# One core, cosine attention and a two-layer product: the hand-written order of steps is permuted from the start to the third batch's second unit

## The chip, the cores and the metric

The kernel runs on one core of a Trainium2 chip. The core has a matrix engine (TensorE, PE in the profile; its loads of weights are PEld), three engines for elementwise work (VectorE: DVE, ScalarE: ACT, GpSimd: POOL), and SyncE (SP), which here only issues DMAs. The metric is device time of one execution in microseconds (us). Three runs of the kernel before took 415.35 us in the median.

## The reference, cut to what matters

```python
q_n = q / (np.linalg.norm(q, axis=-1, keepdims=True) + 1e-06)      # q, k, v: (8, 12, 448, 64) float32
k_n = k / (np.linalg.norm(k, axis=-1, keepdims=True) + 1e-06)
scores = np.matmul(q_n, k_n.transpose(0, 1, 3, 2)) / tau           # tau = 0.1
attn = np.exp(scores - max); attn = attn / (sum(attn) + 1e-09)
x = np.matmul(attn, v).transpose(0, 2, 1, 3).reshape(3584, 768)
h = x @ w_in                                                       # (768, 2048)
out = np.maximum(0.01 * h, h) @ w_out                              # (2048, 768)
```

Eight batches, each with twelve heads of 448 rows and 64 columns; then a product with w_in, a leaky relu and a product with w_out over all 3584 rows.

## The kernel before, in words

The whole kernel is a list of steps, the string `ORDER` (lines 16 to 98). Each step is a name and numbers; a loop (L727) calls one small function for each step, and this function issues its instructions to its engine. Each engine takes its instructions in the order in which they were issued, and waits at each one until its inputs are there and its buffers are free. So `ORDER` fixes one queue for each engine. The relative order of two steps matters only where they are on one engine, or where they take a buffer from one pool.

A *pair* `s` is two heads of one batch (pairs 0 to 5 are batch 0, pairs 6 to 11 batch 1). From pair 12 on, work goes by *units*, and `s` counts the queries and the keys of a unit by turns: 12 and 13 are unit 0, 16 and 17 unit 2.

The steps of a pair, with engine and line:

- `lq.s` (SP, L222) loads queries and keys of a pair; pairs 0 to 5 are loaded ahead of the list (L651 to L659), from SP and, for three loads, ACT. Four buffers hold later pairs, in the order in which `lq` stands in the list. `hs.s` (SP, L700) is a tiny DMA that reads the normalised pair `s` and so holds SP's later DMAs back until `no.s` is done.
- `sq.s.p` squares (POOL, L306 and L300), part 0 the queries, part 1 the keys; for pair 0 and pair 1 ACT does it (`qf` L324, `sa` L304). `su.s.p` sums over columns (DVE, L319, L316; `uf` L330 for pair 0). `ro.s` is a log and an exponential that make a root (ACT, L336, L337). `no.s` normalises into bfloat16 (DVE, L342, L343, L359; L349 from pair 12).
- `tp.s` transposes (PE, L374), `tc.s` copies the result (DVE, L390); for pair 0 in two parts, of which ACT copies one (`ta`).
- `k.s.i` scores (PE, L427), i from 0 to 2; `k.s.3` takes the last 64 keys of pairs s-1 and s together. `x.s.i` is their exponential (ACT, L438).
- Two pairs make a `j`: `to.j` sums the exponentials (PE, L450 with ones), `ln.j` and `in.j` make the inverse (ACT, L462, L466), `pr.j.e` multiplies with the values (PE, L450), `sc.j.e` scales into `xT` (DVE, L478).

For a unit the steps are `tt`, `td` (turned by DVE and spread by six SP DMAs, L400 and L409), `q` and `y` (scores and exponentials, L492 and L500), `g`, `gl`, `gi`, `gx` (sums or products, log, inverse, scaling: L538, L546, L550, L564 and L570).

The products with the weights go by chunks `c` of rows: chunk 0 is 384 rows of batch 0, chunk 1 the other 512 rows of batches 0 and 1. `f.c.m` multiplies with 128 columns of w_in (PE, L588, six matmuls, one for each 128 rows `kt` of w_in; `f.0.1.0.2` does only kt 0 and 2). Rows kt 0 and 1 come from j = 0, 2 and 3 from j = 1, 4 and 5 from j = 2. `r.c.m` is the leaky relu (ACT, L602). `s.c.t.lo.hi` multiplies 128 rows with half of w_out (PE, L624, sixteen matmuls), `o` copies the result (DVE, L640) and, when a row is complete, issues its DMA on SP.

POOL issues the other loads: `wi.i` (L182) a quarter of w_in, 0 and 1 the left half of the columns (m 0 to 7; 0 the even kt, 1 the odd), 2 and 3 the right half; `wo` (L188) w_out, first its left half of columns, then the right half in two quarters; `lv.j` and `lr` the values of batches 0 and 1 (L256, L264); `lg` the values of later groups (L282). `hp.s` (L704) is a tiny copy on POOL that reads the normalised pair `s` and so holds POOL's queue until `no.s` is done; `hr` (L707) waits in the same way for the first load.

PE writes into eight PSUM banks, given out when the list is walked (`take`, L156): the free bank that was given back longest ago. Scores take two banks, everything else one, except `g` with two. Until the step `tg` scores may only have banks 0 to 3 and the rest only 4 to 7; behind it all may have all eight. `w.n` (L695) is n matmuls on a constant tile, whose results nobody reads.

Of the kernel before, what the change touches and what calls it, by code (L numbers as in the profile page):

```python
# [21 lines left out]
k.3.1 x.3.1 pr.0.1 w.2 su.5.0 no.4 lq.9 su.5.1 sc.0.0 hp.4 sq.6.0 sq.6.1 wi.2 k.3.2 x.3.2 w.2 ro.5 tp.4 tc.4  # L22
k.3.3 x.3.3 w.2 k.4.0 x.4.0 k.4.1 x.4.1 to.1 ln.1 in.1 no.5 sc.0.1 hp.5 sq.7.0 sq.7.1 wi.3 k.4.2 x.4.2 tp.5
tc.5 pr.1.0 k.5.0 x.5.0 k.5.1 x.5.1 pr.1.1 sc.1.0 sc.1.1 su.6.0 su.6.1 su.7.0 su.7.1 wo.0 sq.8.0 sq.8.1 lv.3
lr.1.0.4 k.5.2 x.5.2 f.0.0.0.2 f.0.1.0.2 k.5.3 x.5.3 f.0.0.1 f.0.1.1 f.0.0.3 f.0.1.3 tg ro.6 to.2 ln.2 in.2
no.6 pr.2.0 pr.2.1 f.0.2.0.1.2.3 f.0.3.0.1.2.3 sc.2.0 sc.2.1 ro.7 lq.10 sq.9.0 sq.9.1 tp.6 tc.6 f.0.0.4.5
r.0.0 f.0.1.4.5 r.0.1 f.0.2.4.5 r.0.2 f.0.3.4.5 r.0.3 no.7 lq.11 su.8.0 su.8.1 k.6.0 k.6.1 k.6.2 x.6.0 x.6.1
x.6.2 f.0.4 r.0.4 f.0.5 r.0.5 tp.7 tc.7 ro.8 no.8 hp.8 sq.10.0 sq.10.1 lv.4 wo.1.0.8 su.9.0 su.9.1 f.0.6 r.0.6
f.0.7 r.0.7 k.7.0 k.7.1 x.7.0 x.7.1 f.0.8 r.0.8 tp.8 tc.8 ro.9 no.9 hs.9 lq.12 su.10.0 su.10.1 f.0.9 r.0.9
f.0.10 r.0.10 k.7.2 k.7.3 x.7.2 x.7.3 f.0.11 r.0.11 tp.9 tc.9 ro.10 no.10 hp.10 sq.11.0 sq.11.1 wo.1.8 lv.5  # L30
# [734 lines left out]
```

## Time and profile before

| | |
|---|---|
| median of three runs | 415.35 us (414.4 to 415.75) |
| the profiled execution | 415.95 us, with a span of 414.0 us |
| mean granted clock of PE | 1.000 |
| PE busy in the span | 403.3 us |
| DVE, ACT, POOL busy | 261.5, 247.3, 113.6 us |
| DMA | 53.81 MB |

The profile is of one execution. A row of a timeline gives start, duration, engine, line, operation and tiles; "[0.34 <-DVE ...]" is how long the engine was idle before it and what ended this. Times count from the start of the span. A window row gives the busy time of each engine in a stretch. Queue q0 carries the DMAs that POOL issues, q1 those of SP.

### The profile page before, as it was taken

Reading aid. Unit: us, or ns where it says so; the run is one execution under the profiler, and the core shown is the slowest. Engines: PE = TensorE matmul, PEld = TensorE weight load, DVE = VectorE, ACT = ScalarE, POOL = GpSimd, SP = SyncE. Lnnn points to the kernel's source line nnn. Section 1 sums busy time; section 2 is a strip of 40 time slices with the busy share of each in tenths; the row PEclk is TensorE's granted clock in tenths of the full one; section 3 lists DMA queues with packets and bytes.
Section 4 is the critical chain, followed back from the end, with each engine's and each line's share of the span. In section 5 each row is a group of like instructions: output and inputs, shape, how many; then the busy total and the mean of one; then the engine's idle time right before and its main releaser. Section 6 shows DMA issues by size and latency. Waiting matters only on the chain.

```text
span 414.0 us, 11078 instructions
## 1 busy us (share of the span) xinstructions
PE 403.3 (97%) x4662; PEld 211.0 (51%) x4679; DVE 261.5 (63%) x424; ACT 247.3 (60%) x431; POOL 113.6 (27%) x125
## 2 busy tenths in 40 slices
PE   7699999999999999999999999999999999999997
PEld 2235555544555555544455555554455555554465
DVE  6878878656678565765584877599978591310021
ACT  5897877288657786667864769525854735104400
POOL 4785564133235132432240623330010000000000
PEclk9999999999999999999999999999999999999999
DMA  7999999964387842693555756392052210010032
GB/s 184 234 203 220 218 222 201 257 166 114 62 212 193 209 112 56 181 232 98 96 136 159 178 154 165 79 206 83 2 90 78 87 40 0 2 70 7 2 114 76
DMA packets 41976, 53.81 MB, mean 130 GB/s; under 512 B 12486, under 2 KB 32326, under 8 KB 41926
## 3 DMA queue, kind: packets, MB, share of 16 engines
q1 hardware_dynamic: 25734, 41.01, 35.8%
q0 software_dynamic: 15504, 11.80, 19.7%
q8 instruction: 36, 0.59, 0.6%
q10 hardware_dynamic: 688, 0.30, 0.2%
q14 instruction: 14, 0.11, 0.1%
HBM read 45.61 MB, written 11.01 MB: 137 GB/s over the span
## 4 chain that ended last, share of the span: by engine, by line
PE 83%; DMA 6%; DVE 3%; issue 2%; ACT 2%; POOL 2%; SPq 1%; POOLq 0%; DVEq 0%
PE ps L624 33%; PE ps L588 32%; PE ps L538 7%; PE ps L492 6%; DMA qk_h<-in_k_dram 3%; PE ps L450 2%; DMA vq<-in_v_dram 2%; DVE qn L359 1%; DVE ss L319 1%; ACT pe L438 1%; DMA xT<-in_q_dram 1%; PE ps L427 1%; POOL sq L306 1%; SPq L409 1%; PE ps L524 1%
## 5 line engine op out<-in xcount | busy, mean ns | idle before, releaser
L624 PE MATMUL ps<-w_out_sb,hT 128*128 128x384 bf16 (+1 forms) x912 | 151.7, 324 | 0.0
L588 PE MATMUL ps<-xT,w_in_sb 128*128 128x384 bf16 (+1 forms) x753 | 150.3, 352 | 1.0 <-issue 0.3
L500 ACT ACTIVATE pe<-ps 128x896 bf16<-128x896 f32 x126 | 109.2, 917 | 46.8 <-PE ps L492 46.6
L624 PEld LDWEIGHTS <-hT 128*128 128x128 bf16 x912 | 86.4, 98 | 64.4 <-issue 10.7
L588 PEld LDWEIGHTS <-w_in_sb 128*128 128x128 bf16 x768 | 72.9, 98 | 73.5 <-issue 9.0
L602 ACT ACTIVATE hT<-ps 128x384 bf16<-128x384 f32 (+1 forms) x128 | 65.0, 552 | 62.3 <-PE ps L588 44.1
L300 POOL TENSOR_TENSOR sq<-qk_h 128x896 f32<-128x896 f32 x36 | 62.5, 1740 | 60.1 <-DMA qk_h<-in_k_dram 33.6
L640 DVE COPY osb<-ps 128x384 f32<-128x384 f32 (+1 forms) x57 | 30.7, 544 | 76.5 <-PE ps L624 72.9
L349 DVE TENSOR_TENSOR qn<-qk_h,r 128x896 bf16<-128x896 f32 x36 | 42.7, 1186 | 1.6 <-DVE r L343 0.4
L316 DVE TENSOR_REDUCE ss<-sq 128x14 f32<-128x910 f32 x36 | 38.1, 1062 | 1.1 <-POOL sq L300 1.1
L438 ACT ACTIVATE pe<-ps 128x896 bf16<-128x896 f32 x42 | 36.0, 917 | 3.2 <-PE ps L427 3.1
L492 PE MATMUL ps<-qkT 64*32 64x448 bf16 x1008 | 36.0, 352 | 0.3 <-DVE osb L640 0.3
L508 DVE TENSOR_TENSOR shared<-shared,pe 128x896 f32<-128x896 f32 x30 | 35.6, 1218 | 0.3
L564 DVE TENSOR_TENSOR xT<-ps,rb 128x448 bf16<-128x448 f32 x32 | 18.3, 614 | 20.3 <-ACT rb L550 12.4
L400 DVE STREAM_TRANSPOSE tt<-qn 128x448 f32<-128x448 f32 x36 | 29.3, 817 | 0.7
L704 POOL CAST seen<-qn 128x1 f32<-128x1 bf16 x21 | 3.9, 185 | 92.0 <-DVE qn L349 86.0
L342 DVE TENSOR_REDUCE r<-norms 128x14 f32<-128x28 f32 x48 | 8.4, 176 | 31.1 <-ACT norms L337 30.8
L538 PE MATMUL ps<-pe,vq 64*32 64x448 bf16 x1008 | 27.0, 349 | 0.0
L492 PEld LDWEIGHTS <-qkT 64*32 64x32 bf16 x1008 | 12.6, 91 | 19.2 <-issue 15.0
L336 ACT ACTIVATE ss<-ss 128x14 f32<-128x14 f32 x48 | 10.3, 215 | 18.3 <-DVE ss L316 17.2
L282 POOL DMA_DIRECT2D vq<-in_v_dram x20 | 12.7, 639 | 26.6 <-PE ps L492 26.6
L538 PEld LDWEIGHTS <-vq 64*32 64x32 bf16 x1008 | 14.6, 93 | 8.6 <-issue 0.6
(55 smaller groups left out, 234.9 us busy)
## 6 DMA issues: line engine op xcount, KB each, us to landing
qk_h<-in_q_dram SPq DMA_DIRECT2D x36, 224.0 KB, 4.1
qk_h<-in_k_dram SPq DMA_DIRECT2D x36, 224.0 KB, 4.1
out_dram<-osb SPq DMA_DIRECT2D x20, 384.0 KB, 2.6
qkT<-tt SPq DMA_DIRECT2D x72, 56.0 KB, 2.0
qkT<-tt SPq DMA_DIRECT2D x36, 112.0 KB, 2.6
vq<-in_v_dram POOLq DMA_DIRECT2D x16, 224.0 KB, 4.9
w_in_sb<-in_moe_w_in_dram POOLq DMA_DIRECT2D x4, 768.0 KB, 10.9
out_dram<-osb SPq DMA_DIRECT2D x15, 192.0 KB, 3.1
```

Source lines behind the costliest of these rows:

```text
L300: gp.tensor_tensor(sq[:, :, :D], x, x, op=ALU.mult)
L316: nc.vector.tensor_reduce(o, sqs[s], axis=AX.X, op=ALU.add)
L349: nc.vector.tensor_tensor(qn[s].rearrange("p m d e -> p m e d"), raw[s].rearrange(f"p ({t[1:-1]} d) -> p m e d", e=n, d=D), r.rearrange(f" ...
L438: nc.scalar.activation(out=dst, in_=sc[:, :, :S], func=AF.Exp, scale=inv_tau)
L492: nc.tensor.matmul(out=sc[32 * strip : 32 * strip + 32, a, :S], lhsT=x[rows, c0 : c0 + 32], rhs=x[rows, 0:S], start=True, stop=True,)
L500: nc.scalar.activation(out=pq[u, i], in_=sc[:, :, :S], func=AF.Exp, scale=inv_tau)
L508: eng.tensor_tensor(whole[u], pq[u, 0] if i == 1 else whole[u], pq[u, i], op=ALU.add)
L538: nc.tensor.matmul(out=po[32 * strip : 32 * strip + 32, w, :S], lhsT=weights, rhs=pq[us[x if two else 0], i][rows, a, :], start=(i == 0), ...
L588: nc.tensor.matmul(out=pm[:, :n], lhsT=w_in_sb[:, kt, m * 128 : (m + 1) * 128], rhs=xT[c // 2][:, kt, c0 : c0 + n], start=(done + i == 0), ...
L602: nc.scalar.activation(out=hT[c][:, m, :n], in_=pm[:, :n], func=AF.Prelu, alpha=0.01)
L624: nc.tensor.matmul(out=po2[:, : hi - lo], lhsT=hT[c][:, m, ts * 128 : (ts + 1) * 128], rhs=w_out_sb[:, m, lo:hi], start=(m == 0), stop=(m ...
L640: nc.vector.tensor_copy(out=o[:, lo:hi], in_=bank(("s", c, ts, lo))[:, : hi - lo])
```

## The change

Only the string `ORDER` changes. It holds the same 1261 steps, in another order from its first line up to `q.3.2` (the third batch's second unit is the one whose first score steps stand there); behind that point both lists are the same, but for one copy, `o.1.0.384.768`, which moves down to that border. The main moves:

- `tg` moves from the first products with w_in to the first transposes of pair 0.
- POOL: `sq.2` now stands in front of `lr.0` and `lv.0`; `hr` moves behind `lv.2`, `hp.1` behind `sq.4.1`; `lv.1` and the squares of pairs 3 and 4 stand in front of `wi.0` and `wi.1`, which follow each other; `wi.2` and `wi.3` follow each other behind the squares of pair 7; the last quarter of w_out stands behind `sq.13` and `sq.12`.
- SP: `lq.8` stands in front of `hs.3`; `lq.13` in front of `lq.12`; the order behind is `lq.16`, `lq.18`, `lq.19`, `lq.17`.
- ACT and DVE: the parts of pairs are taken in another order, `ro.1` stands in front of `ta.0.0.4`, `no.9` in front of `no.8`, some sums in front of norms that stood ahead of them.
- PE: `f.0.6` and `f.0.15` come forward, the steps `f.1` are mixed, `s.0.2.384.768` stands in front of `s.0.1.384.768`, and some steps of one kind that were apart now follow each other.

The diff, cut to the parts of which the prediction speaks:

```diff
-w.20 qf.0.0.3 uf.0.0.3 qf.1.0.3 uf.1.0.3 qf.0.3.4 uf.0.3.4 ro.0 hr lr.0.0.2 sa.1.1 sa.1.0 no.0 su.1.1 lq.6
-sq.2.0 sq.2.1 lv.0 tp.0.0.4 ta.0.0.4 tp.0.4.7 su.1.0 tc.0.4.7 w.3 ro.1 k.0.0 x.0.0 k.0.1 x.0.1 w.2 no.1 su.2.0
-su.2.1 lq.7 hp.1 sq.3.0 sq.3.1 lr.0.2.4 wi.0 k.0.2 x.0.2 ro.2 tp.1 tc.1 w.2 k.1.0 x.1.0 k.1.1 x.1.1 w.2 no.2
-su.3.0 sq.4.0 sq.4.1 lv.1 wi.1 k.1.2 x.1.2 w.2 tp.2 tc.2 k.1.3 x.1.3 su.3.1 ro.3 w.2 k.2.0 x.2.0 k.2.1 x.2.1
-to.0 ln.0 in.0 su.4.0 no.3 hs.3 lq.8 sq.5.0 sq.5.1 lv.2 su.4.1 k.2.2 x.2.2 tp.3 tc.3 pr.0.0 ro.4 k.3.0 x.3.0
...
+qf.0.0.3 qf.1.0.3 uf.0.0.3 lq.6 qf.0.3.4 w.20 uf.1.0.3 uf.0.3.4 ro.0 sa.1.1 sq.2.1 sa.1.0 no.0 tp.0.4.7 su.1.0
+sq.2.0 su.1.1 tg tp.0.0.4 w.2 lr.0.0.2 ro.1 tc.0.4.7 su.2.1 lv.0 sq.3.1 no.1 su.2.0 w.2 ta.0.0.4 sq.3.0 lq.7
+k.0.1 lr.0.2.4 x.0.1 k.0.0 w.2 w.2 tp.1 k.0.2 x.0.0 w.2 tc.1 k.1.3 ro.2 no.2 su.3.0 su.3.1 x.0.2 k.1.2 x.1.3
+lv.1 k.1.1 x.1.2 x.1.1 ro.3 w.2 sq.4.1 k.1.0 tp.2 w.3 tc.2 k.2.1 k.2.2 k.2.0 x.1.0 su.4.1 to.0 x.2.2 pr.0.0
+no.3 hp.1 sq.4.0 su.4.0 x.2.1 x.2.0 ro.4 tp.3 w.2 wi.0 tc.3 ln.0 wi.1 sq.5.1 k.3.3 lq.8 su.5.1 k.3.2 k.3.1
+sq.5.0 w.2 no.4 su.5.0 hp.4 sq.6.0 x.3.3 lv.2 hr x.3.1 x.3.2 pr.0.1 tp.4 tc.4 k.3.0 ro.5 x.3.0 no.5 in.0 k.4.0
+k.4.1 hp.5 x.4.1 sc.0.0 sc.0.1 to.1 tp.5 k.4.2 ln.1 pr.1.1 pr.1.0 sq.6.1 sq.7.0 sq.7.1 tc.5 x.4.0 in.1 x.4.2
+sc.1.1 k.5.0 sc.1.0 k.5.2 hs.3 x.5.0 k.5.3 wi.2 x.5.2 f.0.1.0.2 f.0.0.0.2 k.5.1 x.5.1 wi.3 su.6.0 su.6.1
+su.7.1 f.0.1.1 f.0.1.3 f.0.0.1 ro.6 x.5.3 sq.8.0 wo.0 lv.3 f.0.2.0.1.2.3 f.0.3.0.1.2.3 to.2 pr.2.1 pr.2.0 lq.9
+ln.2 in.2 no.6 su.7.0 tp.6 sq.8.1 lq.10 sc.2.1 sc.2.0 f.0.6 sq.9.1 f.0.3.4.5 f.0.2.4.5 f.0.0.4.5 r.0.6
+f.0.1.4.5 ro.7 lr.1.0.4 r.0.2 sq.9.0 tc.6 su.8.0 su.8.1 no.7 k.6.2 k.6.0 r.0.3 f.0.4 f.0.5 x.6.2 sq.10.0 tp.7
+lq.11 sq.10.1 tc.7 r.0.1 su.9.0 su.9.1 f.0.0.3 f.0.7 r.0.4 x.6.0 r.0.5 r.0.0 ro.8 f.0.15 k.6.1 k.7.0 ro.9
...
+tp.8 r.0.13 r.0.11 lq.13 r.0.12 wo.1.0.8 r.0.14 k.9.1 tc.8 x.9.1 su.11.1 sq.13 k.9.0 to.3 su.11.0 ln.3 lq.12
+k.9.3 ro.11 k.8.0 x.9.3 x.9.0 x.8.0 tp.10 s.0.0.0.384 no.11 tc.10 k.8.1 k.10.1 k.8.2 sq.12 x.8.1 in.3 pr.3.1
+o.0.0.0.384 wo.1.8 hs.11 su.13 pr.3.0 ro.13 x.8.2 x.10.1 tp.11 s.0.1.0.384 hp.11 tc.11 k.11.0 sc.3.0 lv.5
...
```

More of the change, by code (lines that the diff above doesn't have):

```diff
@@ L22 @@
[L22 to L26, printed above, removed]
@@ new lines @@
+y.1.5 r.1.8 g.0.0 r.1.14 q.2.0 q.1.6 su.21 su.20 s.1.0.0.384 y.1.6 ro.20 ro.21 y.2.0 gx.0.0 q.2.2 q.2.1 q.2.3
+no.21 o.1.0.0.384 tt.19 no.20 lq.22 tt.20 s.1.1.0.384 s.1.0.384.768 tt.21 lq.23 td.3 lq.24 td.4 lq.25
+o.1.1.0.384 sq.23 hp.19 sq.22 y.2.2 lg.1 su.22 y.2.1 q.2.4 y.2.3 hp.20 y.2.4 q.2.5 q.2.6 y.2.5 y.2.6
+s.1.1.384.768 o.1.1.384.768 ro.22 s.1.2.0.384 o.1.2.0.384 no.22 tt.22 lq.26 hp.22 sq.24 su.23 q.3.0 y.3.0 g.1
+gl.1 q.3.1 q.3.2 y.3.1 o.1.0.384.768 y.3.2 gi.1 ro.23 s.1.2.384.768 o.1.2.384.768 no.23 q.3.3 y.3.3 g.1.0
@@ new lines @@
+gx.1.0 tt.23 td.5 lq.27 hp.23 sq.25 su.24 q.3.4 q.3.5 y.3.4 y.3.5 ro.24 s.1.3.0.384 o.1.3.0.384 q.3.6 y.3.6
+g.1.1 gx.1.1 q.4.0 q.4.1 y.4.0 y.4.1 lg.2 s.1.3.384.768 o.1.3.384.768 no.24 tt.24 lq.28 sq.26 su.25 q.4.2
+y.4.2 q.4.3 q.4.4 y.4.3 y.4.4 f.2.0 r.2.0 f.2.1 r.2.1 f.2.2 r.2.2 f.2.3 r.2.3 f.2.4 r.2.4 ro.25 f.2.5 r.2.5
+no.25 tt.25 td.6 lq.29 hp.25 sq.27 su.26 q.4.5 y.4.5 q.4.6 q.5.0 y.4.6 y.5.0 f.2.6 r.2.6 f.2.7 r.2.7 f.2.8
+r.2.8 f.2.9 r.2.9 f.2.10 r.2.10 ro.26 f.2.11 r.2.11 no.26 tt.26 lq.30 hp.26 sq.28 su.27 q.5.1 y.5.1 g.2 gl.2
@@ new lines @@
+q.5.2 q.5.3 y.5.2 y.5.3 gi.2 f.2.12 r.2.12 f.2.13 r.2.13 f.2.14 r.2.14 f.2.15 r.2.15 ro.27 s.2.0.0.384
+o.2.0.0.384 no.27 q.5.4 y.5.4 g.2.0 gx.2.0 tt.27 td.7 lq.31 sq.29 su.28 q.5.5 q.5.6 y.5.5 y.5.6 lg.3 ro.28
+s.2.0.384.768 o.2.0.384.768 no.28 q.6.0 y.6.0 g.2.1 gx.2.1 tt.28 lq.32 hp.28 sq.30 su.29 q.6.1 q.6.2 y.6.1
+y.6.2 ro.29 s.2.1.0.384 o.2.1.0.384 no.29 tt.29 td.8 lq.33 sq.31 su.30 q.6.3 y.6.3 g.3 gl.3 q.6.4 q.6.5 y.6.4
+y.6.5 gi.3 s.2.1.384.768 o.2.1.384.768 ro.30 s.2.2.0.384 o.2.2.0.384 q.6.6 y.6.6 g.3.0 gx.3.0 q.7.0 q.7.1
@@ L66 @@
+f.3.14 r.3.14 ro.34 f.3.15 r.3.15 no.34 q.9.0 y.9.0 g.4.1 gx.4.1 tt.34 lq.38 hp.34 sq.36 su.35 q.9.1 q.9.2
+y.9.1 y.9.2 ro.35 s.3.0.0.384 o.3.0.0.384 no.35 tt.35 td.11 lq.39 hp.35 sq.37 su.36 q.9.3 y.9.3 q.9.4 q.9.5
+y.9.4 y.9.5 s.3.0.384.768 o.3.0.384.768 ro.36 s.3.1.0.384 o.3.1.0.384 q.9.6 y.9.6 q.10.0 q.10.1 y.10.0 y.10.1
 s.3.1.384.768 o.3.1.384.768 s.3.2.0.384 o.3.2.0.384 no.36 tt.36 lq.40 sq.38 su.37 q.10.2 y.10.2 g.5 gl.5
```

55 lines of the change are left out of this document (16 added, 39 removed).

## The prediction

> **What bounds the kernel now.** I read the slices of the page first, then busy time by stage, then the waits of the first 34 us.
>
> ```profile
> PE   7699999999999999999999999999999999999997
> ```
>
> PE is full but for the first two slices or three and the last. In the windows (us, length, busy time of PE, PEld, DVE, ACT, POOL, granted clock, DMA share, GB/s) I put a border at 31.40, where the first product with w_in starts. The second fence holds the warming matmuls (`w`, L695) of the first window alone.
>
> ```profile
> 1.65:31.40 29.75, 25.16 (x220) 9.86 (x222) 23.10 (x52) 23.40 (x42) 21.18 (x28) 1.00 1.08 218
> 31.40:55.76 24.36, 24.30 (x238) 13.20 (x236) 19.98 (x40) 19.70 (x42) 13.99 (x18) 1.00 1.25 220
> ...
> 82.29:125.50 43.21, 43.00 (x516) 20.86 (x512) 29.38 (x47) 31.27 (x55) 13.64 (x14) 1.00 0.57 139
> ```
> ```profile
> 1.65:31.40 29.75, 11.04 (x37) 3.41 (x39) 1.00 1.08 218
> ```
>
> Behind 31.40 PE idles 0.06 us in 24.36 and 0.2 in 43.21. So a gain has to come from an earlier start of that full stretch, and a loss from new waits in it. Ahead of it lie 4.6 us of idle time, 11 of warming, and matmuls that only keep pace with the exponentials on ACT:
>
> ```profile
> 10.03:33.86 23.83, 19.98 (x215) 8.04 (x219) 20.19 (x40) 21.65 (x35) 18.90 (x25) 1.00 1.15 220
> ```
> ```profile
> ACT pe L438 <- PE ps L427: 2.2, 6, 0.6
> ```
>
> From its first exponential (10.03) to the roots of pair 6 (33.86) ACT is busy 21.65 of 23.83 us; the other 2.2 it waits for scores. ACT bounds the start. The DMA engines are full there too (share over 1).
>
> **The change, step by step.** It permutes steps; none is added or dropped, so each engine does the same work, and the ten warming steps stay. What moves is the start of PE's full stretch, and what each step finds ready.
>
> *First exponential, later by 1.0.* The rows of PE, ACT and DVE:
>
> ```profile
> 9.62 0.55 PE L427 MATMUL ps<-qkT 64*128 64x448 bf16 x4 [0.34 <-DVE qkT L390]
> ```
> ```profile
> 7.34 1.04 ACT L304 ACTIVATE sq<-xT 128x384 f32<-128x384 f32 x2 [0.80 <-DMA xT<-in_k_dram]
> 8.29 0.56 ACT L390 COPY qkT<-ps 128x512 bf16<-128x512 bf16 x1
> ...
> 10.03 2.54 ACT L438 ACTIVATE pe<-ps 128x896 bf16<-128x896 f32 x3 [0.23 <-PE ps L427]
> ```
> ```profile
> 8.15 1.15 DVE L319 TENSOR_REDUCE ss<-sq 128x6 f32<-128x390 f32 x2
> ...
> 10.33 1.16 DVE L359 TENSOR_TENSOR qn<-xT,r 128x512 bf16<-128x512 f32 x2
> ...
> 13.58 2.20 DVE L359 TENSOR_TENSOR qn<-xT,r 128x512 bf16<-128x512 f32 x2
> ```
>
> Now `ro.1` stands ahead of `ta.0.0.4`, and the two sums of pair 1 are turned round. `su.1.0` can't start before ACT's squares end (8.38), so both sums end at 8.4+1.15 = 9.6, `ro.1` (0.45) at 10.05 and the copy (0.56) at 10.6. The scores need that copy; 0.4 behind them (9.62 to 10.03 before) the first exponential starts: 11.05 for 10.03.
>
> *Fewer waits, earlier by 1.7.* `tg` now stands near the start, so scores take any free pair of the eight banks instead of two fixed pairs, and run ahead of ACT. I followed ACT's queue by hand with these durations, and of its 2.2 us of waits about 0.5 remain, at `ro.3` and `ro.4`, which wait for DVE: `sq.3` lies beside `no.2` as before (its two multiplications took 2.20 for the 1.16 of `no.1`), and `sq.4.0`, no longer behind a hold that keeps it off, beside a bit of `no.3` (0.2 lost). ACT gets to the roots of pair 6 and `x.5.3` at 11.05+21.65+0.5 = 33.2, for 33.86. Bounds: no wait, 32.7; all 2.2 again, 34.9.
>
> *Start of the w_in products.* `f.0.1.0.2` needs `k.5.3` issued (its banks come from `x.4.2`) and `sc.1.0`. Up to the end of `x.4.2` ACT has 18.0 us of work (17 exponentials at 0.82 from start to start, as in the row of 10.03: 13.9; four pairs of roots at 0.45: 1.8; two logs and two inverses: 2.2): 11.05+18.0+0.5 = 29.5. DVE copies pair 5 until 28.25; `in.1` is there at 28.7, `pr.1.0` at 29.0, `sc.1.0` at 29.9. So w_in's products start at 29.95 for 31.40, with equal work done on PE (`k.5.3` stands ahead in place of `k.5.1`): **1.45 earlier**.
>
> *Does PE stay full?* Prices, from start to start:
>
> ```profile
> 33.99 1.69 PE L450 MATMUL ps<-pe,shared 128*32 128x448 bf16 x32
> ...
> 43.85 0.57 PE L427 MATMUL ps<-qkT 64*64 64x448 bf16 x8
> 44.35 1.15 PE L588 MATMUL ps<-xT,w_in_sb 128*128 128x384 bf16 x6
> 45.34 0.55 PE L374 MATMUL ps<-id,qn 128*128 128x128 bf16 x7
> ```
>
> A strip pass (`to`, `pr`) costs 0.8, a score step 0.25, a w_in matmul 0.163, a transpose step 0.5; with these the second window sums to 24.3 of its 24.36. In the new order all of `f.0.0` to `f.0.7` (48 matmuls, 7.8), three score steps, three passes and two transpose steps (0.75+2.4+1.0) stand between `f.0.1.0.2` and `f.0.15`, which so starts at 29.95+11.95 = 41.9. It is the first to ask for the right half of w_in; before, that was `f.0.8`, at 44.35.
>
> When does this half land? POOL and SP rows, then landing times of first loads and of w_in, then queue q0 in 20:22 and both queues in 32.7:42 (packets, MB, share):
>
> ```profile
> 5.41 0.37 SPq L220 DMA_DIRECT2D xT<-in_k_dram  x1
> ```
> ```profile
> 13.09 2.27 POOL L306 TENSOR_TENSOR sq<-xT 128x512 f32<-128x512 f32 x2 [1.28 <-ACT norms L337]
> 15.31 1.30 POOL L264 DMA_DIRECT2D shared<-in_v_dram  x2
> 16.61 0.77 POOL L182 DMA_DIRECT2D w_in_sb<-in_moe_w_in_dram  x1
> 17.39 1.84 POOL L306 TENSOR_TENSOR sq<-xT 128x512 f32<-128x512 f32 x2
> 19.17 0.81 POOL L256 DMA_DIRECT2D shared<-in_v_dram  x1
> 19.98 0.75 POOL L182 DMA_DIRECT2D w_in_sb<-in_moe_w_in_dram  x1
> ...
> 29.39 0.80 POOL L182 DMA_DIRECT2D w_in_sb<-in_moe_w_in_dram  x1
> 30.19 1.18 POOL L188 DMA_DIRECT2D w_out_sb<-in_moe_w_out_dram  x1
> ```
> ```profile
> DMA to landing us min/median/max: 3.3/4.4/5.9
> ```
> ```profile
> DMA to landing us min/median/max: 7.6/10.9/12.6
> ```
> ```profile
> q0 software_dynamic: 176, 0.36, 105.7%
> ...
> w_in_sb<-in_moe_w_in_dram POOLq DMA_DIRECT2D x1, 768.0 KB, 10.6
> ```
> ```profile
> q0 software_dynamic: 925, 1.52, 88.1%
> q1 hardware_dynamic: 907, 0.51, 25.6%
> ```
>
> The second quarter of w_in, issued at 19.98, landed 10.6 later, at 30.6; the last, issued at 29.39, 12.6 later, at 42.0. POOL's new queue starts with the keys of pair 2 (issued at 5.41 and, at the shortest landing of 3.3, there at 8.7) and puts `lr.0`, `lv.0`, `lv.1` and the squares of pairs 2 to 4 ahead of w_in: 8.7+1.85+1.4+0.8+2.1+1.3+0.8+2.05 = 19.0. So w_in starts 2.4 later than at 16.61, but without `lv.1` in its midst (0.2 MB at 0.163 MB/us, 1.2) and behind the rush of first loads (I take 1.2): the second quarter again lands about 30.6 and is asked for at 30.85. The third and fourth are issued at 29.4 and 30.2, behind `hp.4`, `hp.5` and the squares of pairs 6 and 7. Until then q0 is busy with the second and `lv.2`, which hides the delay, and they land 11.4 behind it as before, at 42.0. **Wait at `f.0.15`: 0.1.** Bounds: none, if w_in runs at the 0.18 MB/us of 20:22; 1.8 by the row of 17:30.55, 1.95 MB in 13.55 us, at which rate w_in and `lv.2` (3.34 MB) run from 20.5 (1.5 behind the issue, an estimate) to 43.7:
>
> ```profile
> q0 software_dynamic: 2087, 1.95, 94.6%
> ```
>
> On SP, `lq.8` no longer stands behind `hs.3`, so `lq.8` and `lq.9` ride beside w_in's first half and `lq.10` beside the second. In 32.7:42 w_in kept 0.163 MB/us beside q1, against 0.18 alone: a loss of a tenth, which is in my numbers. [...]
>
> *Behind it.* w_out's landing, its issue and the first and fourth products with it:
>
> ```profile
> DMA to landing us min/median/max: 15.2/15.5/23.2
> ```
> ```profile
> 54.84 0.94 POOL L188 DMA_DIRECT2D w_out_sb<-in_moe_w_out_dram  x1
> ...
> 57.98 3.31 POOL L300 TENSOR_TENSOR sq<-qk_h 128x896 f32<-128x896 f32 x2
> ```
> ```profile
> 55.76 2.45 PE L624 MATMUL ps<-w_out_sb,hT 128*128 128x384 bf16 x14
> ```
> ```profile
> 71.20 3.10 PE L624 MATMUL ps<-w_out_sb,hT 128*128 128x384 bf16 x18
> ```
>
> The left half of w_out landed at 30.19+23.2 = 53.4. In the new order 0.55 more of work stands ahead of `s.0.0.0.384` (`to.3` and `k.9.3` come forward, `k.8.1` and `k.8.2` go back): 55.76-1.35+0.55 = 55.0, so 1.6 of cover. The last quarter of w_out moves behind `sq.13` and `sq.12`, which wait for loads that wait for `no.8` and `no.9`; if these squares end near 61.3 as before, it is issued then instead of at 54.84. It landed 15.5 later, at 70.3, because q0 was still busy with the quarter ahead of it; that hides the delay. It is asked for at 71.2-1.35+0.8 (`to.5` comes forward), plus 1.35 for the eight weights of the quarter ahead: 72.0. Without that cover it is 1 us per us.
>
> For the rest (sums ahead of norms, `lq.18`, `lq.19`, `lq.17`, the later `td`, the mixed order of `f.1`) I followed banks and inputs: `f.1.12`, with 63.5 us of work ahead, asks at 81.1 for `sc.5.0` of 79.8; elsewhere there are 0.1 to 3 us of cover, thinnest where ACT frees banks for `f.0.9` and `f.0.10` and DVE for `s.0.1.384.768`. Two changes fewer between full-array and strip work gain 0.1; small waits cost between nothing and 1.5, and I take 0.15, near the 0.2 of window 82.29:125.50.
>
> **Sum:** -1.45+0.1+0.15-0.1 = -1.3. The profiled execution took 415.95 (its span of 414.0 and 1.95 around it), so 414.65. The median of the runs lies 0.6 below it: 415.35-1.3 = **414.05**.
>
> **Rivals.** (A) *The front gains nothing.* ACT, starting 1.0 later, waits nearly as long as before, because norms move against squares and DVE (busy 20.19 of 23.83) falls behind; `sc.1.0` comes at 31. Time within 0.5 of before, 415.3. Against it: the scores' new banks. Chance 0.2. (B) *Slower: the right half of w_in lands late.* `f.0.15` moved 10 us of PE work forward, and all of PE stands behind it. Each us past 41.9 costs one; from 43.4 on the whole gain is gone, and at 44.2 to 46 the time is 416 to 418. For it: two quarters issued later behind two holds, loads put ahead. Against it: the rates above. [...] (C) *More gain.* ACT loses its 0.5 of waits and w_in is there by 40: another 0.6 to 1.2, 413.4 to 412.8. Chance 0.1.
>
> **How the numbers follow.** Forecast 0.47, with its own range 413.4 to 414.7. About 0.3%, 1.25 us, is what a measurement can tell from no change. Faster: 0.33 of the forecast, and C: 0.43. Same: the rest of the forecast, A and a bit of B: 0.36. Slower: 0.21. The range, 412.9 to 416.8, leaves out little of C and the worse half of B.
>
> **What would show it.** First exponential at 11.05; ACT idle under 1 us from there to the roots of pair 6 at about 33.2; the first L588 near 29.95; PE idle near 41.9 under 0.5, ended by w_in's DMA if at all; the first L624 near 55.0. I am wrong if L588 starts after 31, or if PE idles over 1 us between 31 and 125.

## The result, and the profile after

The kernel after took 414.77 us in the median of 22 runs, the kernel before 415.61 in 22 runs beside it: a ratio of 0.9981, with a 95% interval of 0.9973 to 0.9990, that is 0.4 to 1.1 us less. The direction is that of the forecast (414.05), the size about two thirds of its 1.3. The profiled execution of after took 414.45, with a span of 412.7 (before: 415.95 and 414.0), a difference of 1.5; the one trace lies 0.3 above the median of its kernel and the other 0.3 below, so that a difference of two traces says too much here. One of the 22 runs of after, at 442.75 us with a granted clock of 0.91, was slow and is not in the ratio.

The busy time of PE in slices, from the page of after:

```profile
PE   7899999999999999999999999999999999999997
```

The windows of after, with the first border where the products with w_in start (columns as before):

```profile
1.65:30.22 28.57, 25.33 (x221) 10.48 (x224) 24.13 (x53) 21.75 (x41) 18.50 (x26) 1.00 1.07 229
30.22:55.46 25.24, 24.88 (x249) 13.52 (x245) 18.89 (x41) 21.04 (x45) 17.22 (x20) 1.00 1.22 216
...
82.14:123.83 41.69, 41.43 (x491) 20.22 (x500) 27.03 (x44) 28.31 (x51) 18.00 (x16) 1.00 0.65 152
```

The start came forward from 31.40 to 30.22, by 1.18 (in rest_alone below, whose front is the old one, it lies at 31.15, so a part of this may be chance). But in the window behind it PE now idles 0.36 of 25.24, where it idled 0.06 of 24.36. The same two kernels over equal work, from the first product with w_in to the border of the change (`q.3.2`), before and then after:

```profile
31.40:125.08 93.68, 93.41 (x1035) 48.07 (x1045) 68.96 (x120) 65.10 (x122) 38.43 (x43) 1.00 0.90 185
```
```profile
30.22:123.83 93.61, 92.92 (x1034) 47.99 (x1042) 67.65 (x119) 65.27 (x123) 44.68 (x46) 1.00 0.90 182
```

PE is busy 0.49 less for the same work, and idle 0.69 for 0.27. So three things have to be told apart: an earlier start, less PE time for the same matmuls, and new waits.

The start of after on ACT, from its timeline and its waits between 10 and 34:

```profile
10.06 0.57 ACT L390 COPY qkT<-ps 128x512 bf16<-128x512 bf16 x1
11.08 1.73 ACT L438 ACTIVATE pe<-ps 128x896 bf16<-128x896 f32 x2 [0.45 <-PE ps L427]
```
```profile
ACT pe L438 <- PE ps L427: 1.0, 2, 0.5
ACT ss L336 <- DVE ss L319: 0.8, 3, 0.4
```

ACT waits less for scores (1.0 for 2.2), but the roots (L336) now wait 0.8 for the sums of DVE.

The first two quarters of w_in, issued at 18.59 and 19.39 (the least value is the first quarter's, the largest the second's), and PE behind them:

```profile
DMA to landing us min/median/max: 8.0/10.0/11.9
```
```profile
30.22 0.82 PE L588 MATMUL ps<-xT,w_in_sb 128*128 128x384 bf16 x4
30.98 0.36 PE L427 MATMUL ps<-qkT 64*128 64x448 bf16 x2
31.38 1.80 PE L588 MATMUL ps<-xT,w_in_sb 128*128 128x384 bf16 x10
```

The second quarter landed at 31.3, just when it was asked for; PE's load of weights waited 0.3 for it. And w_out's left half, issued at 32.45, with the first product that needs it:

```profile
DMA to landing us min/median/max: 23.0/23.0/23.0
```
```profile
55.47 2.77 PE L624 MATMUL ps<-w_out_sb,hT 128*128 128x384 bf16 x16 [0.34 <-DMA w_out_sb<-in_moe_w_out_dram]
```

It landed at 55.4 instead of 53.4, and PE waited 0.34.

### The profile page after: what moved, and what is told of

Read it like the earlier page. It is cut to its first block, busy times and chain, and to the rows that moved or that the text cites. A ratio compares the mean times of both kernels' runs of the same rounds, so it can differ in the third digit from the quotient of the medians.

```text
span 412.7 us, 11078 instructions
## 1 busy us (share of the span) xinstructions
PE 403.0 (98%) x4662; PEld 211.5 (51%) x4679; DVE 262.2 (64%) x424; ACT 245.8 (60%) x431; POOL 117.9 (29%) x125
## 4 chain that ended last, share of the span: by engine, by line
PE 83%; DMA 10%; DVE 3%; SPq 2%; issue 1%; POOL 1%; DVEq 0%
PE ps L624 33%; PE ps L588 32%; PE ps L538 8%; PE ps L492 7%; DMA w_out_sb<-in_moe_w_out_dram 6%; DMA qk_h<-in_q_dram 2%; PE ps L450 2%; DMA qk_h<-in_k_dram 1%; DMA xT<-in_q_dram 1%; DVE shared L508 1%; PE ps L524 1%; PE ps L427 1%; SPq L211 0%; SPq L219 0%; DVE qn L359 0%
## 5 line engine op out<-in xcount | busy, mean ns | idle before, releaser
L624 PE MATMUL ps<-w_out_sb,hT 128*128 128x384 bf16 (+1 forms) x912 | 151.7, 324 | 0.3 <-DMA w_out_sb<-in_moe_w_out_dram 0.3
L588 PE MATMUL ps<-xT,w_in_sb 128*128 128x384 bf16 (+1 forms) x753 | 149.4, 352 | 1.1 <-issue 0.5
L624 PEld LDWEIGHTS <-hT 128*128 128x128 bf16 x912 | 86.4, 98 | 64.3 <-issue 10.1
L588 PEld LDWEIGHTS <-w_in_sb 128*128 128x128 bf16 x768 | 73.2, 98 | 73.4 <-issue 7.8
L300 POOL TENSOR_TENSOR sq<-qk_h 128x896 f32<-128x896 f32 x36 | 64.8, 1805 | 77.6 <-DMA qk_h<-in_q_dram 39.5
L349 DVE TENSOR_TENSOR qn<-qk_h,r 128x896 bf16<-128x896 f32 x36 | 43.9, 1220 | 1.5
L704 POOL CAST seen<-qn 128x1 f32<-128x1 bf16 x21 | 6.6, 315 | 68.9 <-DVE qn L349 66.1
L342 DVE TENSOR_REDUCE r<-norms 128x14 f32<-128x28 f32 x48 | 8.3, 174 | 21.7 <-ACT norms L337 21.1
L336 ACT ACTIVATE ss<-ss 128x14 f32<-128x14 f32 x48 | 10.3, 215 | 9.4 <-DVE ss L316 6.3
```

The source lines that it names most:

```text
L300: gp.tensor_tensor(sq[:, :, :D], x, x, op=ALU.mult)
L349: nc.vector.tensor_tensor(qn[s].rearrange("p m d e -> p m e d"), raw[s].rearrange(f"p ({t[1:-1]} d) -> p m e d", e=n, d=D), r.rearrange(f" ...
L588: nc.tensor.matmul(out=pm[:, :n], lhsT=w_in_sb[:, kt, m * 128 : (m + 1) * 128], rhs=xT[c // 2][:, kt, c0 : c0 + n], start=(done + i == 0), ...
L624: nc.tensor.matmul(out=po2[:, : hi - lo], lhsT=hT[c][:, m, ts * 128 : (ts + 1) * 128], rhs=w_out_sb[:, m, lo:hi], start=(m == 0), stop=(m ...
```

## The experiments

The theory that I started with: the gain is the earlier start, and it shrinks at the late landings. The rival: the gain comes from the rest of the new order. In front_alone, rest_alone, hold_pair8 and copy_first, and only there, the list fills six lines less, so that line numbers are six smaller (L582 is L588, L618 is L624, L421 is L427). Ratios are to the kernel before, run beside each, whose median stands in the third column. They are taken over all the runs and are not the quotient of the two medians: where some runs are long, as in w_in_early, the two differ.

| kernel | median | before beside it | ratio | 95% interval |
|---|---|---|---|---|
| front_alone | 415.99 | 415.78 | 1.0012 | 0.9984 to 1.0041 |
| rest_alone | 414.82 | 415.78 | 0.9973 | 0.9958 to 0.9989 |
| hold_pair8 | 415.10 | 415.78 | 0.9969 | 0.9948 to 0.9990 |
| copy_first | 414.51 | 415.78 | 0.9973 | 0.9951 to 0.9996 |
| after_again | 414.69 | 415.58 | 0.9980 | 0.9967 to 0.9993 |
| visits_split | 417.11 | 415.58 | 1.0043 | 1.0028 to 1.0058 |
| hold_lq8 | 414.85 | 415.58 | 0.9985 | 0.9969 to 1.0002 |
| banks_alone | 415.56 | 415.58 | 0.9997 | 0.9978 to 1.0016 |
| w_in_early | 415.76 | 415.85 | 1.0016 | 0.9995 to 1.0038 |
| combined | 415.68 | 415.85 | 1.0002 | 0.9994 to 1.0011 |
| values_first | 418.76 | 415.85 | 1.0064 | 1.0041 to 1.0086 |
| front_lv5 | 414.62 | 415.57 | 0.9977 | 0.9956 to 0.9998 |

**front_alone.** The old list up to its `tg` is the front; its steps stand in the new order, and behind them the old list goes on.

```diff
-w.20 qf.0.0.3 uf.0.0.3 qf.1.0.3 uf.1.0.3 qf.0.3.4 uf.0.3.4 ro.0 hr lr.0.0.2 sa.1.1 sa.1.0 no.0 su.1.1 lq.6
+qf.0.0.3 qf.1.0.3 uf.0.0.3 lq.6 qf.0.3.4 w.20 uf.1.0.3 uf.0.3.4 ro.0 sa.1.1 sq.2.1 sa.1.0 no.0 tp.0.4.7 su.1.0
...
 ro.6 to.2 ln.2 in.2
```

> The new order only for the steps that stand before the first four products with w_in in the old list; the old order behind. Theory (the whole gain is an earlier start of the products with w_in, because ACT waits less for scores): the first exponential at 11.1, the first product with w_in at 30.2 (31.40 before, 30.22 after), the left half of w_out lands about 23 us behind its issue, near 53.5, and nothing waits for it; time 1.1 to 1.3 below before, about 414.4. Rival (the gain hangs on the rest: fewer visits, f.0.6 and f.0.15 forward): the start comes earlier, but PE stalls behind it, and the time is within 0.4 of before.

The start came even earlier than expected, at 29.79, but the gain in time did not come: four of twelve runs took 418.6 to 419.6 (mean granted clock 0.996), the others 414.5 to 416.5 (0.999 or 1.00). The kernel before has such runs too, three of the 36 beside it. The profiled run is one of the long ones. POOL of this kernel, its DVE, then its windows (the column before the last two is the granted clock):

```profile
59.15 0.75 POOL L250 DMA_DIRECT2D shared<-in_v_dram  x1 [4.33 <-PE ps L444]
...
60.04 3.32 POOL L294 TENSOR_TENSOR sq<-qk_h 128x896 f32<-128x896 f32 x2
```
```profile
61.77 1.10 DVE L310 TENSOR_REDUCE ss<-sq 128x14 f32<-128x910 f32 x1 [3.61 <-POOL sq L294]
62.78 0.61 DVE L384 COPY qkT<-ps 128x896 bf16<-128x896 bf16 x1
```
```profile
60.00:62.00 2.00, 1.12 (x18) 0.25 (x9) 0.23 (x1) 0.03 (x1) 2.00 (x3) 1.00 1.26 252
62.00:64.00 2.00, 0.55 (x7) 0.15 (x6) 2.00 (x4) 1.07 (x3) 1.36 (x1) 0.77 1.13 256
64.00:66.00 2.00, 2.00 (x11) 0.83 (x8) 1.93 (x4) 1.80 (x3) 0.00 (x0) 0.50 1.16 232
66.00:68.00 2.00, 2.00 (x12) 1.08 (x10) 1.89 (x3) 0.04 (x1) 1.82 (x2) 0.87 1.31 204
68.00:70.00 2.00, 2.00 (x21) 0.96 (x20) 1.65 (x4) 1.78 (x4) 0.00 (x0) 1.00 1.23 167
```

The load of values `lv.5` stood on POOL for 4.3 us. The row names the products with values (L444) as what ended it; the chain of the trace leads further back, to the landing of `lv.3` at 58.61, for which these products waited too. The squares of pair 12 stood behind it, the sum of pair 12 waited for them on DVE, and behind this sum stood the copy of pair 11 for which PE waited 2.33 us. Then PE ran two more us at half its clock.

**rest_alone.** The other half: the old front, the new order behind it.

```diff
 f.0.0.3 f.0.1.3 tg
-ro.6 to.2 ln.2 in.2
+ro.6 f.0.2.0.1.2.3 f.0.3.0.1.2.3 to.2 pr.2.1 pr.2.0
```

> The old order up to the first four products with w_in, the new one behind. Theory: the first product with w_in at 31.4 as before, and no gain: between -0.2 and +0.4 of before. Rival (part of the gain is in the larger visits or in the mixed order of the products): 0.4 or more faster with an unchanged start.

It is 0.5 to 1.7 us faster than before, with the start at 31.15: the rival holds for this half. The stretch of equal work in this kernel:

```profile
31.15:124.34 93.19, 92.79 (x1035) 48.08 (x1044) 70.17 (x119) 64.19 (x122) 41.27 (x43) 1.00 0.88 181
```

PE is busy 0.62 less than in the same stretch of before, and idle 0.40 for 0.27: not fewer waits, but fewer PE microseconds for the same matmuls.

**visits_split.** Between the first product with w_in and the border, PE goes from products with the weights or transposes (128*128 in the rows) to scores and strip passes, or back, 38 times before and 34 times after: two visits less. Seven more visits:

```diff
-q.0.4 q.0.3 q.0.5 su.18 su.17 td.1 y.0.3 hp.15 lg.0 f.1.7 r.1.1 ro.16 no.16 y.0.4 r.1.7
+q.0.4 q.0.3 su.18 su.17 td.1 y.0.3 hp.15 lg.0 f.1.7 r.1.1 ro.16 no.16 y.0.4 r.1.7 q.0.5
...
```

> The kernel after, with seven score steps (q.0.1, q.0.5, q.1.0, q.1.2, q.2.3, k.7.3, k.6.0) moved a step or two down, each behind one product with a weight, so that between the first product with w_in and the border of the change PE goes 52 times from products with the weights to other matmuls or back, for 38 after and 48 before. Theory (the fewer changes are what the rest of the new order gains; from the traces so far a visit, which is two changes, costs 0.1 to 0.3): the time is 0.7 to 2.1 above the kernel after, PE stays busy, and the stretch from the first product with w_in to the border gets longer by this. Rival (my prediction's price of 0.05 for a change, and the gain of the rest lies elsewhere, in waits): 0.7 or less.

(The 38, 48 and 52 in this text count transposes as other work; without them they are 34, 38 and 48.) The time is 2.4 above that of after_again beside it, more than my theory's upper end. The same stretch, first in visits_split, then in after_again:

```profile
30.70:126.90 96.20, 94.81 (x1035) 47.88 (x1042) 69.93 (x119) 65.65 (x123) 43.02 (x46) 1.00 0.87 178
```
```profile
30.04:123.81 93.77, 92.75 (x1033) 48.00 (x1041) 68.38 (x119) 65.38 (x123) 44.65 (x46) 1.00 0.89 182
```

PE is busy 2.06 longer for the same matmuls: 0.29 a visit. How it comes about is to be seen where one visit of three score steps became two, in visits_split and then in after_again:

```profile
87.37 0.57 PE L492 MATMUL ps<-qkT 64*32 64x448 bf16 x16
87.88 1.47 PE L588 MATMUL ps<-xT,w_in_sb 128*128 128x512 bf16 x6
89.27 0.38 PE L492 MATMUL ps<-qkT 64*32 64x448 bf16 x8
89.82 3.83 PE L588 MATMUL ps<-xT,w_in_sb 128*128 128x512 bf16 x17 [0.16 <-issue]
```
```profile
86.31 0.76 PE L492 MATMUL ps<-qkT 64*32 64x448 bf16 x24
87.01 5.35 PE L588 MATMUL ps<-xT,w_in_sb 128*128 128x512 bf16 x23
```

From start to start, three steps in one visit take 0.70; two and one take 0.51 and 0.55 (0.39 without the 0.16 of idle time), and the six products between them 1.39 instead of 1.30 (at 0.216 for a product with 512 columns: the visit of 24 in the last row, of which the trace lacks one, takes 3.88 more than the visit of six, for 18 more). So 0.3 more for the same work, 0.45 with the idle time. Two visits less at 0.29 would be 0.6, and PE needs 0.5 to 0.7 less in after, after_again and rest_alone. Single traces scatter by nearly as much: over this stretch PE is busy 92.8 to 93.3 in seven kernels with the new rest and no step of PE moved, and 93.2 to 93.7 in three with the old rest (all at full clock). That the two visits are this gain is worked out from the price of seven added ones; no run takes away two alone.

**after_again.** The kernel after once more, as the measure for visits_split, hold_lq8 and banks_alone, which were run beside it.

> The kernel after, unchanged, as the measure for the kernels beside it, and for a second trace of where its time goes. Expected: 0.1 to 0.3% faster than before; the first product with w_in at 30.2 to 30.4; and, if the landing of the second quarter of w_in varies from run to run as it did between four traces of this front (31.3 to 32.8), a wait of 0.2 to 1.3 us at the first product with kt 1.

The ratio is that of the first measurement. Its trace starts the products with w_in at 30.04 and waits longer for the second quarter:

```profile
31.86 1.31 PE L588 MATMUL ps<-xT,w_in_sb 128*128 128x384 bf16 x7 [0.71 <-DMA w_in_sb<-in_moe_w_in_dram]
```

**hold_pair8.** One word of the kernel after:

```diff
-no.8 hs.9 no.10
+no.8 hs.8 no.10
```

> The kernel after, with one step changed: the hold on SP in front of the load of pair 13 reads pair 8 and not pair 9, so that SP's queue is held 3 to 4 us longer. Theory (w_out's left half came 2 us late because the load of pair 13, with its large packets, rode beside it from 46 on): that load is issued near 50, w_out's left half lands at 53.5 to 54.2 (55.42 after), PE no longer waits for it at the first product with w_out (0.34 after), and the time is 0.2 to 0.5 below the kernel after. Rival (w_out was late for another reason, or the load of pair 13 is now late itself): the landing stays within 0.5 of 55.4, or a wait at the transposes of pair 13 takes the place, and the time is not below that of the kernel after.

SP's hold in after, and in hold_pair8; then both queues between 50 and 52, in the same order (packets, MB, share):

```profile
45.45 0.64 SPq L701 DMA_DIRECT2D behind<-qn  x1
46.18 1.64 SPq L230 DMA_DIRECT2D qk_h<-in_k_dram  x2
```
```profile
52.16 0.64 SPq L695 DMA_DIRECT2D behind<-qn  x1
```
```profile
q0 software_dynamic: 268, 0.21, 65.8%
q1 hardware_dynamic: 136, 0.37, 56.3%
```
```profile
q0 software_dynamic: 522, 0.38, 123.0%
q1 hardware_dynamic: 94, 0.02, 8.8%
```

Without pair 13's load q0 moves 0.38 MB where it moved 0.21. w_out landed 20.8 behind its issue at 32.60, at 53.4, and nothing waited for it (combined, with the same hold, has 20.8 too; five kernels with the hold and w_out as in after have 21.7 to 22.4, and in none of them did PE wait for it):

```profile
DMA to landing us min/median/max: 20.8/20.8/20.8
```

The mechanism is as expected; the gain can't be told in time, since the intervals of this kernel and of after overlap. In this run PE had lost more at the second quarter of w_in, which landed only at 32.8:

```profile
32.82 1.47 PE L582 MATMUL ps<-xT,w_in_sb 128*128 128x384 bf16 x8 [1.34 <-DMA w_in_sb<-in_moe_w_in_dram]
```

**copy_first.**

```diff
-su.1.0 sq.2.0 su.1.1 tg tp.0.0.4 w.2 lr.0.0.2 ro.1 tc.0.4.7 su.2.1 lv.0 sq.3.1 no.1 su.2.0 w.2 ta.0.0.4
+su.1.1 su.1.0 sq.2.0 tg tp.0.0.4 w.2 lr.0.0.2 ta.0.0.4 ro.1 tc.0.4.7 su.2.1 lv.0 sq.3.1 no.1 su.2.0 w.2
```

> The kernel after, with ACT's copy of pair 0's transposes ahead of the roots of pair 1, and the sums of pair 1 in the old order. Theory A (ACT bounds the front): the first exponential comes back to 10.0 or 10.1, ACT has 1 us more time, the first product with w_in starts at 29.2 to 29.6, and up to 1.0 of time is gained on the kernel after. Theory B (DVE bounds it, since the norms are slowed beside POOL's squares and feed the transposes): ACT's gained microsecond turns into waits for scores, and the products start at 30.0 to 30.3, with 0 to 0.3 of gain.

ACT of this kernel:

```profile
9.73 1.73 ACT L432 ACTIVATE pe<-ps 128x896 bf16<-128x896 f32 x2 [0.21 <-PE ps L421]
12.99 0.21 ACT L330 ACTIVATE ss<-ss 128x14 f32<-128x14 f32 x1 [1.54 <-DVE ss L313]
```

The first exponential is 1.35 earlier than in after, and at the next roots 1.54 go into a wait for DVE's sums. The products with w_in started at 30.30, as in after: theory B. The time (414.51) is within the interval of after.

**banks_alone.** The kernel before, with `tg` ahead of the first transposes.

```diff
-lv.0 tp.0.0.4 ta.0.0.4
+lv.0 tg tp.0.0.4 ta.0.0.4
...
-f.0.0.3 f.0.1.3 tg ro.6
+f.0.0.3 f.0.1.3 ro.6
```

> The kernel before, with the step that frees the banks moved from the first products with w_in to the first transposes, and nothing else. My prediction's mechanism (ACT waits for scores because they have two fixed pairs of banks): ACT's 2.2 us of waits for scores between 10 and 34 fall to about 1, the roots of pair 6 end at 33.0 for 33.86, and the products with w_in start up to 0.8 earlier, in time 0 to 0.8 below before. Rival (the waits come from DVE's norms and copies, which the scores wait for; the free banks only let PE run ahead): waits and start as before within 0.3, time within 0.4 of before.

ACT waits 1.5 us for scores between 9.6 and 34 instead of 2.2, 0.5 for sums and 0.4 for a strip pass; the products start at 30.79 in its trace. In time nothing is to be seen, with 0.9 less to 0.7 more as the interval. So in this trace the free banks move ACT's waits (2.4 in all, for 2.2) rather than remove them; whether they bring the start forward by some 0.3 (30.79, for 31.15 in rest_alone, which does not have them there) stays open.

**hold_lq8** and **w_in_early**: two attempts to bring the second quarter of w_in in time.

```diff
-wi.1 sq.5.1 k.3.3 lq.8 su.5.1
+wi.1 sq.5.1 k.3.3 su.5.1
...
-hs.3 x.5.0
+hs.3 lq.8 x.5.0
```

> The kernel after, with the load of pair 8 back behind SP's hold on pair 3, as before. Theory (the second quarter of w_in comes 0.7 us or more too late since the loads of pairs 8 and 9 ride beside it from 16 us on): it lands at 30.3 to 30.8 as in the kernel before, PE no longer waits at the first product with kt 1, and the time is 0.3 to 0.6 below that of the kernel after. Rival (it is late since it is issued behind more loads and squares on POOL): it lands at 31.2 or later, and the time is that of the kernel after within 0.3.

```diff
-lv.1 k.1.1 x.1.2 x.1.1 ro.3 w.2 sq.4.1
+lv.1 wi.0 wi.1 k.1.1 x.1.2 x.1.1 ro.3 w.2 sq.4.1
...
```

> The kernel after, with the first two quarters of w_in moved up on POOL, from behind the squares of pair 4 (and the hold in front of them) to right behind the first load of values of the second pair group; they are issued 2 to 2.5 us earlier. Theory (what is left of the earlier start is eaten at the first product with kt 1, for which the second quarter of w_in lands at 31.1 to 32.8 and not at 30.6): it lands at 29 to 30.5, the wait of 0.2 to 1.3 us there is gone, and the time is 0.3 to 0.6 below that of the kernel after, about 0.3% below before. Rival (queue q0 is full to the brim from the first loads on, so an earlier issue lands no earlier): it lands at 31 or later, and the time is that of the kernel after within 0.3.

In hold_lq8 it landed at 31.1 with a wait of 0.2, and the time is that of after: the rival. In w_in_early POOL had issued both quarters by 17.96, and the squares came later:

```profile
16.47 1.49 POOL L182 DMA_DIRECT2D w_in_sb<-in_moe_w_in_dram  x2
17.98 0.84 POOL L306 TENSOR_TENSOR sq<-xT 128x384 f32<-128x384 f32 x1
```
```profile
DMA to landing us min/median/max: 10.1/11.9/13.8
```
```profile
ACT ss L336 <- DVE ss L319: 2.4, 2, 2.0
```

Issued 2.1 earlier, the second quarter still landed at 31.0, 13.8 behind its issue (11.9 in after): in this run the landing did not follow the issue. In after the square of pair 4 stood ahead of both:

```profile
16.69 0.84 POOL L306 TENSOR_TENSOR sq<-xT 128x384 f32<-128x384 f32 x1
```

In w_in_early it was 1.3 later (17.98), which made ACT wait 2.4 for sums where it waited 0.8 in after, so that the products started at 31.05. Neither theory had this: in this run the front hung on POOL's squares and DVE's sums. But the later start did not cost the gain in this run. Nothing waited for the second quarter, the stretch up to `q.3.2` ended at 124.04 for 123.81 in after_again, and both profiled runs took 414.77. This run is the fastest of its twelve; five others took 416.7 to 419.1, two of them with a mean granted clock of 0.996. None of these was traced, so where the median lost 1.0 us against after stays open.

**combined.** w_in_early, hold_pair8, and the transposes of pair 9 moved into the visit of `k.7.2`.

```diff
-f.0.9 no.9 tp.9 r.0.9 r.0.10 tc.9 su.10.0 f.0.8 k.7.2 k.9.2 k.7.3
+f.0.9 no.9 r.0.9 r.0.10 su.10.0 f.0.8 tp.9 tc.9 k.7.2 k.7.3
...
```

> The kernel after with three edits: the first two quarters of w_in earlier as in the run beside it; the hold in front of the load of pair 13 on pair 8; and one change of work less on PE (the transposes of pair 9 go into the visit of k.7.2 and k.7.3, and k.9.2 into the next). Theory (a visit costs 0.35 from seven visits added for 2.4; the wait for w_in 0.2 to 1.3; the wait for w_out 0 to 0.35): 0.6 to 1.2 below the kernel after, that is 413.4 to 414.1, about 0.4% below before. Rival (earlier transfers bring new waits, or DVE's later copy of pair 9 holds PE): the time of the kernel after within 0.3, or above it.

The expectation failed: as long as before. The start is late (31.18), as in w_in_early, but that alone cost little there. The visit that I took away was one of transposes, and no price of entering one is to be seen: in the rows of before that the prediction quotes, the six products from 44.35 to the transposes at 45.34 take 0.99, for the 0.98 of six, and the transposes take 0.39 up to the next row:

```profile
45.73 2.11 PE L588 MATMUL ps<-xT,w_in_sb 128*128 128x384 bf16 x12
```

And new losses came: three visits to score steps, near 55, 64 and 94, took 0.4, 0.5 and 0.4 longer than the same steps in w_in_early. In the first two PE waited 0.17 and 0.34 for ACT, which frees banks later in this order; the third shows no wait, and its cause stays open.

**values_first.** Rival B made real: the values of batch 1 ahead of the right half of w_in.

```diff
-hs.3 x.5.0 k.5.3 wi.2
+hs.3 x.5.0 k.5.3 lv.3 lr.1.0.4 wi.2
```

> The kernel after, with the loads of the values of batch 1 that follow w_out put ahead of the right half of w_in (as my rival B has it: loads put ahead make this half late). Theory (all of PE stands behind f.0.15, so each us past its start costs one): the last quarter of w_in lands 1.5 to 2.5 later, near 44, PE waits 1.3 to 2.2 us at f.0.15, and the time is 1.3 to 2.2 above the kernel after. Rival (w_out moves back too, and its landing decides; or the values now come earlier and give some back): the wait at f.0.15 is under 1 us, or the first product with w_out waits for a us or more behind it.

```profile
45.46 0.76 PE L588 MATMUL ps<-xT,w_in_sb 128*128 128x384 bf16 x2 [2.99 <-DMA w_in_sb<-in_moe_w_in_dram]
```
```profile
44.00:46.00 2.00, 0.54 (x2) 0.26 (x3) 1.14 (x2) 0.00 (x0) 0.00 (x0) 0.89 1.27 217
46.00:48.00 2.00, 2.00 (x16) 0.66 (x14) 0.00 (x0) 0.49 (x1) 0.00 (x0) 0.50 1.22 217
48.00:50.00 2.00, 2.00 (x17) 0.91 (x10) 0.00 (x0) 1.88 (x3) 1.29 (x2) 0.76 1.23 230
```

The right half landed at 45.4, and PE waited 3.0 at `f.0.15`. There are four runs. Two kept their clock (1.00 and 0.999) and took 417.5 and 418.0, which is 2.7 and 3.3 above after (414.77): the wait. Two took 419.5 and 420.5 with a mean clock of 0.996, the last of them the one traced here: the wait, and a clock at half behind it. Rival B's price, one us for each us of lateness, holds without the clock, of which it had nothing.

**front_lv5.** front_alone with one step moved, so that POOL's squares no longer stand behind the late values:

```diff
-wo.1.8 lv.5 lq.13
+wo.1.8 lq.13
...
-hp.11 sq.12 sq.13
+hp.11 sq.12 sq.13 lv.5
```

> The kernel with the new order in front alone, and one more step moved: the load of values lv.5 goes from ahead of the squares of pairs 12 and 13 to behind them, because in the trace of the front alone this load waited on POOL until the values lv.3 had landed at 58.6, the squares stood behind it, and PE lost 2.3 us at 61 and more by a lower granted clock. Theory (the earlier start is real, 0.6 to 1.2 less what the wait for the second quarter of w_in takes, and what hid it in the front alone were these stalls): the first product with w_in at 29.8 to 30.4, no wait of PE above 1 us between 33 and 125, no runs 3 us above the rest, and the time 0.2 to 1.0 below before. Rival (the front gains nothing in time, and all that the change gains is in the fewer changes of PE's work): within 0.3 of before or slower, though the stalls are gone.

The theory: 0.1 to 1.8 us faster than before, all eleven runs between 414.1 and 416.3. The load now stands behind the squares:

```profile
56.56 0.18 POOL L704 CAST seen<-qn 128x1 f32<-128x1 bf16 x1 [2.06 <-DVE qn L359]
56.70 3.40 POOL L300 TENSOR_TENSOR sq<-qk_h 128x896 f32<-128x896 f32 x2
60.04 0.82 POOL L256 DMA_DIRECT2D shared<-in_v_dram  x1
```

So the front with this step does gain. In the whole change this step is moved too (`lv.5` stands behind `sq.12` and `sq.13`). That the stall alone hid the gain is not shown: the eight shorter runs of front_alone, with the clock at full speed, lie only 0.2 below the median of before, and none of them was traced. Nor was `lv.5` moved alone in the old order, so a part of the 0.95 may be this step's.

## Why the prediction was right, and where it was not

- *First exponential at 11.05.* It came at 11.08. But it cost nothing: with it 1.35 earlier (copy_first) ACT waited for the sums instead.
- *"ACT bounds the start."* This step failed. ACT is busiest (20.94 of the 22.43 us from 11.08 to 33.51 in after, DVE 20.01, POOL 19.52), but its roots wait for DVE's sums (0.8 in after, 2.4 in w_in_early), and these for POOL's squares: a square 1.3 later started the products 0.8 to 1.0 later (w_in_early against after and after_again), while an earlier ACT changed nothing (copy_first). The 0.5 of waits that I left to ACT were 1.8 in after.
- *Start of the products with w_in, 1.45 earlier.* 1.18 in the trace of after and 1.36 in after_again: right in kind, 0.1 to 0.3 too large in these two. Seven other traces with this front and w_in issued as in after start between 29.47 and 30.70. The front is worth 0.95 in time (0.1 to 1.8), by front_lv5.
- *"The second quarter again lands about 30.6 and is asked for at 30.85."* Mis-sized. It landed at 31.3 in after, 31.8 in after_again and 32.8 in hold_pair8, and PE waited 0.3, 0.7 and 1.3; in six more traces with these issues it waited 0.2 to 0.5. The cover of 0.25 was thinner than the scatter of the landing, and while the landing stays where it is, an earlier start only lengthens this wait. w_in_early, which starts 1.0 later than after_again and does not wait, ends the stretch only 0.2 later. In after_again PE idles 1.02 between 31 and 125, just past the 1 us that the prediction gave as a sign of being wrong. How much of the median this wait takes is not shown.
- *Right half of w_in at 42.0, wait 0.1.* It landed at 41.9 in after, and PE did not wait. Rival B, to which I gave 0.23, did not come. Its price held in the two runs of values_first that kept their clock, and was about 2 us too low in the two that did not. The counts of packets of q0 and q1 stand in no fixed ratio: 925 and 907 in 32.7:42 of before, 268 and 136 between 50 and 52 in after, 522 and 94 there in hold_pair8.
- *"The left half of w_out landed at 53.4 ... so 1.6 of cover."* Failed. I took the landing over from before and had only its new issue in the sum. The hold on pair 9 ended at 45.45, since `no.9` now stands ahead of `no.8`, and pair 13's load rode beside w_out: 55.4, no cover, a wait of 0.34. hold_pair8 showed it. In after_again it landed at 54.7, and PE did not wait, so that the wait is not in every run.
- *"Two changes fewer between full-array and strip work gain 0.1."* Mis-sized and miscounted: I looked at strip passes alone, and no run shows the 0.05 for a change behind this term of the sum. What visits_split showed is 0.29 for a visit, which is two changes. With the scores there are four changes less, two visits at 0.29: 0.6. This would be about half of the 1.1 (0.5 to 1.7) that rest_alone gains; the other half has no account here.
- *The sum of -1.3.* Put together from the trace of after: start -1.18, less work of PE -0.49, more idle time in the stretch +0.42, in all -1.25. The forecast had nearly this sum from a start too early, visits too cheap and waits too short. That these errors nearly cancel in this trace is luck. In the medians the gain is 0.8.

What stays open: the two halves alone gain 0.95 (0.1 to 1.8) and 1.1 (0.5 to 1.7), together 0.8 (0.4 to 1.1). Shared waits could explain that (the whole order waits for the second quarter of w_in and for w_out's left half, rest_alone for neither), but with these intervals the gap may also be chance.

No version here is measurably faster than the kernel after.

## What to carry to other kernels

Count how often the matrix engine goes from full-array products to narrower work and back, scores included: in a stretch where it is full, each visit that was added here was paid at once (0.29 us, the mean of the seven in visits_split), and one saved should be a gain that no late transfer takes back, though no run shows this alone. An earlier start is worth only what the transfers behind it have as cover: here I counted on 0.25 for the second quarter of w_in, it landed at 31.3, 31.8 and 32.8 in three traces, and PE waited 0.3, 0.7 and 1.3. So write the cover beside every transfer, with the queue that shares it, and hold it against the scatter of its landing, which was 1.5 us in these three. When one half of a change gains nothing alone, look in its trace for the step of the other half that protects it.

## What the runs showed of the hardware

Behind two waits of PE, of 2.33 us in front_alone and of 2.99 us in values_first, the granted clock was lower for a while. In slices of 2 us from the one in which PE comes back it was 0.77, 0.50, 0.87 and 1.00 in front_alone, and 0.89, 0.50, 0.76 and 1.00 in values_first. The three slices with a lower clock add up to at most (0.23 + 0.50 + 0.13) x 2 = 1.7 us lost in front_alone, an estimate from these clocks. In the 4 us from 60 to 64, up to the half clock, PE was busy 1.67 there; in the 4 us from 42 to 46 of values_first it was busy 1.01. It does not come every time: two of the four runs of values_first kept a mean clock of 0.999 and 1.00. The longest of the shorter waits behind the start of the products with w_in, 1.34 us in hold_pair8, left the mean clock of its run at 1.000.

A visit to score steps cost 0.29 us beyond the steps themselves, in the mean of the seven that visits_split adds; for one to transposes the rows quoted of before show nothing (0.99 for the six products ahead of it, where six take 0.98).
